# Sixty-four-row products for scores and turned probabilities, and pooled keys without masks

## The chip, the cores and the metric

The kernel runs on one core of one Trainium2 chip. The time is the device time of one launch in microseconds (us), a median over runs. Engines are named as the profile names them: PE is the matrix engine (a matmul is a weight load, on row PEld, and a stream of columns, on row PE), DVE the vector engine, ACT the scalar engine, POOL the general-purpose engine, SP the engine that issues most transfers.

## The reference

Three stages follow each other: attention over pooled keys and values, a weighted sum of four expert networks, and a gated network. Only the first is touched by the change.

```python
def _attn_ref(q, k, v):                      # (4, 8, 576, 64) each
    B, H, S, D = q.shape
    pool = 8
    Sp = S // pool                           # 72
    scale = 1.0 / np.sqrt(D)
    k_p = k.reshape(B, H, Sp, pool, D).mean(axis=3)
    v_p = v.reshape(B, H, Sp, pool, D).mean(axis=3)
    scores = scale * np.matmul(q, k_p.transpose(0, 1, 3, 2))
    scores = scores - np.max(scores, axis=-1, keepdims=True)
    attn = np.exp(scores)
    attn = attn / (np.sum(attn, axis=-1, keepdims=True) + 1e-09)
    return np.matmul(attn, v_p).astype(np.float32)

x = attn_out.transpose(0, 2, 1, 3).reshape(2304, 512)
x = _moe_ref(x, ...)                         # 4 experts, 512 -> 1024 -> 512
return _moe2_ref(x, ...)                     # two gates, a product, two more matmuls
```

## The kernel before

The 2304 tokens are worked on as 18 tiles of 128 (`t`), three tiles to a block of 384 (`i`, six blocks). A batch has 576 tokens, so tiles 4 and 13 hold the end of one batch and the beginning of the next; the helper `segments` cuts them in two halves of 64 tokens.

For a batch, `pool_k` sums eight rows of k for each of the 8 x 72 = 576 pooled rows, which lie in five chunks (`c`, four of 128 rows and one of 64), on DVE by one reduce or on POOL by three additions (the first four chunks of batch 1). The sum is then written twice side by side, once times a mask of even heads and once times a mask of odd heads (`mk`, made at the start); this is a product on POOL, or for three chunks of batch 1 a pair of scaled copies on ACT (`mask_k`). `make_kT` turns the chunks on PE, so that kT holds 128 rows: 64 rows of the even head above 64 rows of the odd head, with zeros where the head is not the column's. The last chunk of 64 rows is filled up with zeros to 128.

`scores(t)` (L530) then makes four products of 128 rows: the queries of a pair of heads are the weights (128 rows, 128 tokens) and 144 columns of kT stream through, 72 for each of the two heads. Heads 0 to 3 go into one PSUM bank and 4 to 7 into a second. The data are plain float32, and each product is two passes on PE (two weight loads and two streams): 8 passes for a whole tile, 16 for one that is cut in halves. `exps` takes the maximum of each bank on DVE and the exponential on ACT, `sums` and `normalise` follow, and `attn_T` (L575) turns the probabilities: eight transposes of 128 rows and 72 columns against the identity, one pass each, four into each of two banks, which ACT copies out (L578). `attend` (L587) multiplies with the pooled values: weights of 72 rows and 64 columns, two heads side by side in the two halves of the output's partitions. Its result is x, the input of the experts.

The order of the work is written out by hand. A list `lead` holds what runs before the first expert: pooling of batch 0, tiles 0 to 2 and their attend, the first weights. After that PE works on the experts' products (L174 to L176: three float32r passes of 384 or 512 columns), and `hooks` puts the rest of the attention between them: scores and exps of tile t at hook `at[t]`, its turn two hooks after the next tile's scores, attend of block i at the front of hook 10 i + 4, which is the hook of scores of tiles 7, 10, 13 and 16, so that these scores stand right behind an attend. The kT of batches 1, 2 and 3 stands at its own places. Everything of the attention is done by 180 us of the span; from there the experts go on, and then the gated network.

PSUM banks for the attention come from `bank`, a ring over eight banks that the experts' products use too.

Of the kernel before, what the change touches and what calls it, by code (L numbers as in the profile page):

```python
# [17 lines left out]
def fused_kernel(  # L18
# [16 lines left out]
    nc = tc.nc  # L35
# [295 lines left out]
    with tc.manual_schedule():  # L331
# [5 lines left out]
            ("at", (H // 2) * BLK * 4, 2), ("e", H * NK * 4, 3), ("kT", NCH * P * 4, 2), ("vp", H * D * 4, 2), ("qT", NP * P * 4, 1),  # L337
            ("kp", D * 4, 4), ("mx", H * 4, 2), ("sm", H * 4, 3), ("hm", NCH * H * 4, 1), ("mk", NCH * 2 * 4, 1),
# [14 lines left out]
        hm = ap.tile([P, NCH, H], F32, tag="hm", name="hm", bufs=1)  # L353
        nc.gpsimd.memset(hm, 1.0)
        nc.gpsimd.affine_select(out=hm, in_=hm, pattern=[[P, NCH], [-NK, H]], compare_op=ALU.is_ge,
                                fill=0.0, base=0, channel_multiplier=1)
        nc.gpsimd.affine_select(out=hm, in_=hm, pattern=[[-P, NCH], [NK, H]], compare_op=ALU.is_ge,
                                fill=0.0, base=NK - 1, channel_multiplier=-1)
        mk = ap.tile([P, NCH, 2], F32, tag="mk", name="mk", bufs=1)
        nc.vector.tensor_reduce(mk, hm.rearrange("p c (a b) -> p c b a", b=2), axis=AX.X, op=ALU.add)  # L360

# [49 lines left out]
        def pool_k(b, c, eng=nc.vector):  # L411
            if c == 0:
                kb_t[b] = ap.tile([P, NCH, 2, D], F32, tag="kb", name="kb", bufs=1)
            r, n = in_t.pop(("k", b, c))
            kp = ap.tile([P, D], F32, tag="kp", name="kp")
            if n < P and b == 0:
                nc.gpsimd.memset(kb_t[b][n:, c], 0.0)
# [18 lines left out]
        kp_t = {}  # L436

        def mask_k(c):
            for a in range(2):
                nc.scalar.activation(kb_t[1][:, c, a], kp_t[c], AF.Copy, scale=mk[:, c, a:a + 1])  # L440

        def make_kT(b, g0, g1):
# [8 lines left out]
            nc.scalar.activation(kT_t[b][:, g0 * P:g1 * P], pt[:, :(g1 - g0) * P], AF.Copy, scale=LOGIT)  # L451
# [71 lines left out]
        def scores(t):  # L523
            qT = qT_t.pop(t)
            sc_t[t] = []
# [136 lines left out]
        def weight(eng):  # L662
            return [(None, lambda: stream.split(eng))]
# [898 lines left out]
```

## Time and profile before

| what | value |
|---|---|
| median of 3 runs | 1148.17 us (1147.83 to 1148.45) |
| the profiled execution's own time | 1147.9 us |
| its span, first to last instruction | 1146.1 us |
| PE busy | 1139.6 us (99%) |
| DVE, POOL, ACT busy | 793.1, 416.8, 376.0 us |
| share of PE in the chain that ended last | 96% |
| granted TensorE clock in the 40 slices | full in all |

The profile gives the instructions of one execution. Starts of matmuls are recorded and their ends are modelled, so what a matmul costs in a row of them is read from the distance between starts. A row of the timeline gathers equal instructions that follow each other: with n of them, a duration d of the whole row and a duration s of one, the distance from start to start is (d - s) / (n - 1).

### The profile page before, as it was taken

Reading aid. Unit: us, or ns where it says so; the run is one execution under the profiler, and the core shown is the slowest. Engines: PE = TensorE matmul, PEld = TensorE weight load, DVE = VectorE, ACT = ScalarE, POOL = GpSimd, SP = SyncE. Lnnn points to the kernel's source line nnn. Section 1 sums busy time; section 2 is a strip of 40 time slices with the busy share of each in tenths; the row PEclk is TensorE's granted clock in tenths of the full one; section 3 lists DMA queues with packets and bytes.
Section 4 is the critical chain, followed back from the end, with each engine's and each line's share of the span. In section 5 each row is a group of like instructions: output and inputs, shape, how many; then the busy total and the mean of one; then the engine's idle time right before and its main releaser. Section 6 shows DMA issues by size and latency. Waiting matters only on the chain.

```text
span 1146.1 us, 17173 instructions
## 1 busy us (share of the span) xinstructions
PE 1139.6 (99%) x5985; PEld 1032.0 (90%) x5985; DVE 793.1 (69%) x1456; ACT 376.0 (33%) x672; POOL 416.8 (36%) x381
## 2 busy tenths in 40 slices
PE   8999999999999999999999999999999999999998
PEld 7898888999899898989898989989889999999997
DVE  7776544867768598658679578877786675774554
ACT  5643432345313053504134421314353313230110
POOL 6765213334525166524336642515001111331211
PEclk9999999999999999999999999999999999999999
DMA  9965515445966726495854578785476165947341
GB/s 229 229 148 123 186 62 197 166 152 183 322 220 196 235 80 181 142 316 167 263 152 123 182 237 192 238 208 146 145 195 230 43 261 209 333 152 288 112 166 56
DMA packets 211555, 213.85 MB, mean 187 GB/s; under 512 B 86596, under 2 KB 166796, under 8 KB 211468
## 3 DMA queue, kind: packets, MB, share of 16 engines
q1 hardware_dynamic: 211180, 212.23, 59.6%
q8 instruction: 47, 0.77, 0.3%
q10 hardware_dynamic: 288, 0.52, 0.1%
q14 instruction: 40, 0.33, 0.1%
HBM read 140.87 MB, written 71.83 MB: 186 GB/s over the span
## 4 chain that ended last, share of the span: by engine, by line
PE 96%; DVE 1%; POOL 1%; ACT 1%; DMA 0%; issue 0%; POOLq 0%
PE g L176 18%; PE g L174 18%; PE g L175 18%; PE s L174 13%; PE s L175 13%; PE s L176 13%; PE sc L530 1%; PE x_ps L587 1%; PE at_ps L575 1%; ACT ap L549 0%; DVE ap L419 0%; DMA stxh<-in_k_dram 0%; DVE ap L543 0%; POOL stxh L422 0%; POOL stxh L421 0%
## 5 line engine op out<-in xcount | busy, mean ns | idle before, releaser
L1014 DVE TENSOR_TENSOR plain<-s,plain 128x384 f32<-128x384 f32 x300 | 158.4, 554 | 83.5 <-PE s L176 35.4
L180 POOL TENSOR_TENSOR round<-x5l,round 128x768 fp32r<-128x768 f32 x60 | 112.2, 1870 | 271.5 <-ACT round L179 254.6
L176 PE MATMUL s<-xo,wl 128*128 128x384 f32 x624 | 208.6, 334 | 0.0
L174 PE MATMUL s<-xo,wh 128*128 128x384 f32 x624 | 208.6, 334 | 0.0
L175 PE MATMUL s<-xo,wh 128*128 128x384 f32 x624 | 208.5, 334 | 0.0
L174 PE MATMUL g<-w2l,round 128*128 128x512 f32 x522 | 204.8, 392 | 0.0
L176 PE MATMUL g<-w2h,round 128*128 128x512 f32 x522 | 203.8, 390 | 0.0
L175 PE MATMUL g<-w2h,round 128*128 128x512 f32 x522 | 203.5, 390 | 0.0
L174 PEld LDWEIGHTS s<-xo,wh 128*128 128x128 f32 x624 | 117.1, 188 | 0.5
L175 PEld LDWEIGHTS s<-xo,wh 128*128 128x128 f32 x624 | 117.1, 188 | 0.5
L176 PEld LDWEIGHTS s<-xo,wl 128*128 128x128 f32 x624 | 117.1, 188 | 0.0
L176 PEld LDWEIGHTS g<-w2h,round 128*128 128x128 f32 x522 | 97.9, 188 | 20.7
L174 PEld LDWEIGHTS g<-w2l,round 128*128 128x128 f32 x522 | 98.0, 188 | 20.0 <-issue 0.8
L175 PEld LDWEIGHTS g<-w2h,round 128*128 128x128 f32 x522 | 98.0, 188 | 19.4
L292 POOL TENSOR_TENSOR x5l<-x5l,x5h 128x256 uint32<-128x256 uint32 x80 | 60.6, 757 | 136.6 <-DVE x5h L291 128.3
L1018 ACT ACTIVATE plain<-s 128x384 f32<-128x384 f32 x60 | 29.2, 487 | 231.4 <-PE s L176 195.5
L179 ACT ACTIVATE round<-x5l 128x768 fp32r<-128x768 f32 x60 | 50.9, 848 | 147.7 <-DVE x5l L1422 146.6
L180 POOL TENSOR_TENSOR round<-plain,round 128x768 fp32r<-128x768 f32 (+1 forms) x29 | 52.5, 1812 | 117.7 <-ACT round L179 101.7
L286 DVE TENSOR_SCALAR x5l<-x5h 128x256 uint32<-128x256 uint32 x80 | 52.9, 662 | 50.3 <-DMA gate<-x5l 28.9
L1014 DVE TENSOR_TENSOR x5l<-s,plain 128x384 f32<-128x384 f32 x120 | 65.6, 556 | 24.8 <-PE s L176 18.3
L1260 ACT ACTIVATE plain<-plain 128x768 f32<-128x768 f32 x36 | 30.5, 848 | 111.3 <-DVE plain L1014 111.3
L174 PE MATMUL g<-xl,round 128*128 128x384 f32 x192 | 66.1, 344 | 0.0
(257 smaller groups left out, 2211.8 us busy)
## 6 DMA issues: line engine op xcount, KB each, us to landing
xo<-keptx SPq DMA_DIRECT2D x42, 768.0 KB
raw<-in_moe_w_dram SPq DMA_DIRECT2D x54, 256.0 KB
keptx<-xo SPq DMA_DIRECT2D x12, 768.0 KB
x5h<-in_moe_w_dram SPq DMA_DIRECT2D x128, 64.0 KB
x5h<-in_moe_w_dram SPq DMA_DIRECT2D x32, 256.0 KB
ob<-acc SPq DMA_DIRECT2D x24, 256.0 KB
kept<-xo SPq DMA_DIRECT2D x8, 768.0 KB
xo<-kept SPq DMA_DIRECT2D x8, 768.0 KB
```

What stands on the lines that cost most here:

```text
L174: nc.tensor.matmul(ps, lh, rl, start=first, stop=False)
L175: nc.tensor.matmul(ps, lh, rh, start=False, stop=False)
L176: nc.tensor.matmul(ps, ll, rh, start=False, stop=last)
L179: nc.scalar.activation(hi, src, AF.Copy)
L180: (lo_eng or nc.vector).tensor_tensor(lo, src, hi.bitcast(F32), op=ALU.subtract)
L286: nc.vector.tensor_scalar(au, h, 0x7FFFFFFF, None, op0=ALU.bitwise_and)
L292: nc.gpsimd.tensor_tensor(au, au, l, op=ALU.add)
L530: nc.tensor.matmul(sc[off:off + n, (hp % 2) * W:(hp % 2 + 1) * W], qT[:, hp, off:off + n], kT_t[b][:, hp * W:(hp + 1) * W], start=True, st ...
L575: nc.tensor.transpose(pt[:NK, g * P:(g + 1) * P], e[:, half * G + g, :], ident)
L1014: nc.vector.tensor_tensor(to, one, two, op=ALU.add)
L1018: nc.scalar.activation(x, product(j, A11, B11), AF.Copy)
L1260: nc.scalar.activation(r, r, AF.Relu)
```

## The change

The masks go. `pool_k` adds in three steps on either engine (256, 128 and twice 64 columns), and the last step writes the sum twice side by side, unmasked. `mask_k` and its copies on ACT go, and the products with the mask. kT therefore holds the same 64 rows twice, and the last chunk is turned with its 64 rows alone (64 rows of weights, 64 columns of identity).

`scores(t)` makes eight products of 64 rows: even heads from partitions 0 to 63 into one bank, odd heads from partitions 64 to 127 into the other, 72 columns each, in turn. `attn_T(t)` makes sixteen transposes of 64 rows: the first 64 tokens of a head into one bank, the last 64 into the other, in turn, 64 columns of identity each. Both banks of a tile are therefore filled together. The order of heads in the probabilities becomes even heads, then odd heads, and `attend` reads it so. The turn of a tile is now one piece; the line that put half of tile 4's turn one hook later goes.

```diff
-            ("at", (H // 2) * BLK * 4, 2), ("e", H * NK * 4, 3), ...
-            ("kp", D * 4, 4), ("mx", H * 4, 2), ("sm", H * 4, 3), ("hm", NCH * H * 4, 1), ("mk", NCH * 2 * 4, 1),
+            ("at", H * BLK * 4, 1), ("e", H * NK * 4, 3), ...
+            ("mx", H * 4, 2), ("sm", H * 4, 3),
...
         def pool_k(b, c, eng=nc.vector):
...
-            if eng is nc.vector:
-                eng.tensor_reduce(kp[:n], r[:n, :].rearrange("p (r d) -> p d r", d=D), axis=AX.X, op=ALU.add)
-            else:
-                eng.tensor_tensor(r[:n, :256], r[:n, :256], r[:n, 256:], op=ALU.add)
-                eng.tensor_tensor(r[:n, :128], r[:n, :128], r[:n, 128:256], op=ALU.add)
-                eng.tensor_tensor(kp[:n], r[:n, :64], r[:n, 64:128], op=ALU.add)
-            if b == 1 and c < NCH - 2:
-                kp_t[c] = kp
-                return
-            (eng if b == 1 else nc.gpsimd).tensor_tensor(kb_t[b][:n, c], kp[:n].unsqueeze(1).broadcast_to([n, 2, D]),
-                                    mk[:n, c].unsqueeze(2).broadcast_to([n, 2, D]), op=ALU.mult)
+            kb = kb_t[b][:n, c]
+            for m in (256, 128):
+                eng.tensor_tensor(r[:n, :m], r[:n, :m], r[:n, m:2 * m], op=ALU.add)
+            one, two = (r[:n, m:m + D].unsqueeze(1).broadcast_to([n, 2, D]) for m in (0, D))
+            eng.tensor_tensor(kb, one, two, op=ALU.add)
...
-        def mask_k(c):
-            for a in range(2):
-                nc.scalar.activation(kb_t[1][:, c, a], kp_t[c], AF.Copy, scale=mk[:, c, a:a + 1])
...
             for c in range(g0, g1):
-                nc.tensor.transpose(pt[:, (c - g0) * P:(c - g0 + 1) * P],
-                                    kb_t[b][:, c].rearrange("p a d -> p (a d)"), ident)
+                n = min(P, NROW - c * P)
+                nc.tensor.transpose(pt[:, (c - g0) * P:(c - g0) * P + n],
+                                    kb_t[b][:n, c].rearrange("p a d -> p (a d)"), ident[:n, :n])
...
         def scores(t):
-            for half in range(2):
-                sc = bank("sc")
-                for hp in range(2 * half, 2 * half + 2):
-                    for off, n, b, s in segments(t * P, P):
-                        nc.tensor.matmul(sc[off:off + n, (hp % 2) * W:(hp % 2 + 1) * W],
-                                         qT[:, hp, off:off + n], kT_t[b][:, hp * W:(hp + 1) * W],
+            sc_t[t] = [bank("sc") for _ in range(2)]
+            for hp in range(NP):
+                for off, n, b, s in segments(t * P, P):
+                    for a, sc in enumerate(sc_t[t]):
+                        nc.tensor.matmul(sc[off:off + n, hp * NK:(hp + 1) * NK], qT[a * D:(a + 1) * D, hp, off:off + n],
+                                         kT_t[b][a * D:(a + 1) * D, (2 * hp + a) * NK:(2 * hp + a + 1) * NK],
                                          start=True, stop=True)
...
-        def attn_T(t, half):
+        def attn_T(t):
...
-            pt = bank("at_ps")
-            for g in range(G):
-                nc.tensor.transpose(pt[:NK, g * P:(g + 1) * P], e[:, half * G + g, :], ident)
...
+            pts = [bank("at_ps") for _ in range(2)]
+            R = P // 2
+            for g in range(H):
+                for n, pt in enumerate(pts):
+                    rows = slice(n * R, (n + 1) * R)
+                    nc.tensor.transpose(pt[:NK, g * R:(g + 1) * R], e[rows, g, :], ident[rows, rows])
...
-        hooks[at[TPB + 2] + 3][:0] = [hooks[at[TPB + 2] + 2].pop()]
```

In the lead, PE's rows from the first scores to the attend of block 0 (sc are the banks of scores, at_ps those of the turned probabilities, vp_ps sums of values, x_ps the attend), before:

```order
L530 MATMUL sc<-ap_72,plain 128x144 x4
L509 MATMUL qT_ps<-ident,stxh 128x128 x4
L530 MATMUL sc<-ap_72,plain 128x144 x8
L469 MATMUL vp_ps<-stxl,ident 72x192 x8
L575 MATMUL at_ps<-ident,ap_72 72x128 x8
L469 MATMUL vp_ps<-stxl,ident 72x64 x8
L575 MATMUL at_ps<-ident,ap_72 72x128 x16
L587 MATMUL x_ps<-ap_72 64x384 x8
```

And after:

```order
L505 MATMUL sc<-ap_72,plain 128x72 x8
L485 MATMUL qT_ps<-ident,stxh 128x128 x4
L505 MATMUL sc<-ap_72,plain 128x72 x16
L445 MATMUL vp_ps<-stxl,ident 72x192 x8
L552 MATMUL at_ps<-ident,ap_72 72x64 x16
L445 MATMUL vp_ps<-stxl,ident 72x64 x8
L552 MATMUL at_ps<-ident,ap_72 72x64 x32
L564 MATMUL x_ps<-ap_72 64x384 x8
```

No group has moved; scores and turns have twice the products, each with half the columns.

Among the experts, PE's rows around the kT of batch 1 (kT_ps; the g are the experts' banks), before:

```order
L174 MATMUL g_491<-xl,round 128x384
L175 MATMUL g_491<-xh,round 128x384
L176 MATMUL g_491<-xh,round 128x384
L447 MATMUL kT_ps<-ident,plain 128x128 x5
L174 MATMUL g_524<-w2l,round 128x512
```

And after:

```order
L174 MATMUL g_525<-xl,round 128x384
L175 MATMUL g_525<-xh,round 128x384
L176 MATMUL g_525<-xh,round 128x384
L422 MATMUL kT_ps<-ident,plain 128x128 x4
L422 MATMUL kT_ps<-ident,plain 128x64
L174 MATMUL g_558<-w2l,round 128x512
```

The last of the five transposes has become one of 64 rows, in the same place.

On ACT, between the attend of block 0 (xh) and the exponentials of tile 3, before (L440 is `mask_k`):

```order
L179 ACTIVATE xh<-x_ps 128x384 x4
L179 ACTIVATE round<-raw 128x512
L440 ACTIVATE plain<-ap_72 128x64 x2
L745 ACTIVATE round<-g_408 128x384
L179 ACTIVATE round<-raw 128x512
L179 ACTIVATE w2h<-raw 128x512
L440 ACTIVATE plain<-ap_72 128x64 x4
L549 ACTIVATE ap_72<-sc,ap_72 128x72 x8
```

And after:

```order
L179 ACTIVATE xh<-x_ps 128x384 x4
L179 ACTIVATE round<-raw 128x512
L720 ACTIVATE round<-g_441 128x384
L179 ACTIVATE round<-raw 128x512
L179 ACTIVATE w2h<-raw 128x512
L523 ACTIVATE ap_72<-sc,ap_72 128x72 x8
```

The six masked copies are gone from in front of the exponentials, and with them ACT's wait for the pooling on POOL.

## Rows read from the trace of the kernel before

**Rows 1.** From the page: span, PE's busy time, the chain that ended last.
```profile
span 1146.1 us, 17173 instructions
...
PE 1139.6 (99%) x5985; PEld 1032.0 (90%) x5985; DVE 793.1 (69%) x1456; ACT 376.0 (33%) x672; POOL 416.8 (36%) x381
...
PE 96%; DVE 1%; POOL 1%; ACT 1%; DMA 0%; issue 0%; POOLq 0%
```

**Rows 2.** Groups by line and shape, PE: count, busy us, mean ns of one.
```profile
L575 PE MATMUL at_ps<-ident,ap 128*72 128x128 f32 x144 | 18.8, 272 | 0.2 <-ACT ap L549 0.2
L530 PE MATMUL sc<-ap 128*128 128x144 f32 x104 | 15.5, 291 | 0.2 <-ACT ap L578 0.2
...
L469 PE MATMUL vp_ps<-stxl,ident 72*72 72x64 f32 x16 | 1.2, 227 | 0.0
```

**Rows 3.** Timeline of PE: scores at 111 us, turn at 116 us (start, length).
```profile
111.00 0.39 PE L176 MATMUL g<-w2h,round 128*128 128x512 f32 x1
111.23 1.14 PE L530 MATMUL sc<-ap 128*128 128x144 f32 x8
...
116.41 1.03 PE L575 MATMUL at_ps<-ident,ap 128*72 128x128 f32 x8
...
117.51 0.40 PE L175 MATMUL g<-w2h,round 128*128 128x512 f32 x1
```

**Rows 4.** Timeline of PE: an attend, then scores of the cut tile 13.
```profile
119.11 0.39 PE L176 MATMUL g<-w2h,round 128*128 128x512 f32 x1
119.43 2.80 PE L587 MATMUL x_ps<-ap 72*64 72x384 f32 x16
122.06 1.15 PE L530 MATMUL sc<-ap 128*64 128x144 f32 x16
...
123.47 0.39 PE L175 MATMUL g<-w2h,round 128*128 128x512 f32 x1
```

**Rows 5.** Timeline of PEld, the weight loads, in the same stretch.
```profile
119.42 0.20 PEld L587 LDWEIGHTS x_ps<-ap 72*64 72x64 f32 x4 [0.35 <-issue]
119.80 0.14 PEld L587 LDWEIGHTS x_ps<-ap 72*64 72x64 f32 x2 [0.18 <-issue]
120.12 0.14 PEld L587 LDWEIGHTS x_ps<-ap 72*64 72x64 f32 x2 [0.18 <-issue]
...
123.14 0.19 PEld L174 LDWEIGHTS g<-w2l,round 128*128 128x128 f32 x1 [0.20 <-issue]
123.25 0.19 PEld L175 LDWEIGHTS g<-w2h,round 128*128 128x128 f32 x1
```

**Rows 6.** Timeline of PE: sums of values in the lead, weights of 72 columns.
```profile
17.44 1.20 PE L469 MATMUL vp_ps<-stxl,ident 72*72 72x64 f32 x16
```

**Rows 7.** Timeline of PE: the kT of batch 2.
```profile
78.75 0.71 PE L447 MATMUL kT_ps<-ident,plain 128*128 128x128 f32 x5
```

**Rows 8.** Timeline of the lead and after: pooling of k, first scores, what POOL waits for.
```profile
4.41 2.92 DVE L419 TENSOR_REDUCE ap<-stxh 128x64 f32<-128x512 f32 x3 [2.10 <-DMA stxh<-in_k_dram]
...
9.27 0.39 POOL L427 TENSOR_TENSOR plain<-ap 64x128 f32<-64x128 f32 x1 [0.27 <-DVE ap L419]
...
10.44 1.22 PE L530 MATMUL sc<-ap,plain 128*128 128x144 f32 x8
...
11.21 0.95 DVE L543 TENSOR_REDUCE ap<-sc 128x4 f32<-128x288 f32 x2 [0.91 <-PE sc L530]
...
13.62 0.72 POOL L461 TENSOR_TENSOR stxl<-stxl 72x256 f32<-72x256 f32 x1 [0.88 <-DMA stxl<-in_v_dram]
...
16.86 1.15 POOL L566 TENSOR_TENSOR ap<-ap 128x576 f32<-128x576 f32 x1 [0.48 <-DVE ap L561]
...
26.89 0.69 DVE L180 TENSOR_TENSOR round<-raw,round 128x512 fp32r<-128x512 f32 x1
...
28.67 0.59 ACT L440 ACTIVATE plain<-ap 128x64 f32<-128x64 f32 x2 [0.82 <-POOL ap L423]
...
30.20 0.28 DVE L427 TENSOR_TENSOR plain<-ap 64x128 f32<-64x128 f32 x1
```

More of the change, by code (lines that the diff above doesn't have):

```diff
@@ L350, in bank @@
             return spare[(turn[0] - 1) % len(spare)](name)
[L353 to L360, printed above, removed]
         staging = [home.tile([P, 3, 512], F32, tag=f"x{i}{t}", name="stx" + t) for i in (NB - 1, NB - 2, NB - 3) for t in "hl"]
@@ L412, in pool_k @@
             if c == 0:
-                kb_t[b] = ap.tile([P, NCH, 2, D], F32, tag="kb", name="kb", bufs=1)
+                kb_t[b] = ap.tile([P, NCH, 2, D], F32, tag="kb", name="kb")
             r, n = in_t.pop(("k", b, c))
-            kp = ap.tile([P, D], F32, tag="kp", name="kp")
-            if n < P and b == 0:
-                nc.gpsimd.memset(kb_t[b][n:, c], 0.0)
-            if eng is nc.vector:
-                eng.tensor_reduce(kp[:n], r[:n, :].rearrange("p (r d) -> p d r", d=D), axis=AX.X, op=ALU.add)
-            else:
-                eng.tensor_tensor(r[:n, :256], r[:n, :256], r[:n, 256:], op=ALU.add)
-                eng.tensor_tensor(r[:n, :128], r[:n, :128], r[:n, 128:256], op=ALU.add)
-                eng.tensor_tensor(kp[:n], r[:n, :64], r[:n, 64:128], op=ALU.add)
-            if b == 1 and c < NCH - 2:
-                kp_t[c] = kp
-                return
-            (eng if b == 1 else nc.gpsimd).tensor_tensor(kb_t[b][:n, c], kp[:n].unsqueeze(1).broadcast_to([n, 2, D]),
-                                    mk[:n, c].unsqueeze(2).broadcast_to([n, 2, D]), op=ALU.mult)
+            kb = kb_t[b][:n, c]
[3 more added lines that the diff above has]
+            eng.tensor_tensor(kb, one, two, op=ALU.add)
         warm_ps = []
@@ L566, in normalise @@
                 eng.tensor_tensor(e_t[t][:, some], e_t[t][:, some], sm_t[t][:, some].unsqueeze(2).broadcast_to([P, h[1] - h[0], NK]), op=ALU.mult)
-        def attn_T(t, half):
+        def attn_T(t):
             i, o = divmod(t, TPB)
             if o == 0:
-                at_t[i, half] = ap.tile([P, G, BLK], F32, tag="at", name="at")
+                at_t[i] = ap.tile([P, H, BLK], F32, tag="at", name="at")
             e = e_t[t]
-            pt = bank("at_ps")
-            for g in range(G):
-                nc.tensor.transpose(pt[:NK, g * P:(g + 1) * P], e[:, half * G + g, :], ident)
-            src = pt[:NK].rearrange("p (g s) -> p g s", s=P)
-            dst = at_t[i, half][:NK, :, o * P:(o + 1) * P]
-            nc.scalar.activation(dst, src, AF.Copy)
+            pts = [bank("at_ps") for _ in range(2)]
[4 more added lines that the diff above has]
+                    nc.tensor.transpose(pt[:NK, g * R:(g + 1) * R], e[rows, g, :], ident[rows, rows])
+            for n, pt in enumerate(pts):
+                at = o * P + n * R
+                nc.scalar.activation(at_t[i][:NK, :, at:at + R], pt[:NK].rearrange("p (g s) -> p g s", s=R), AF.Copy)
         def attend(i, hp):
@@ L587, in attend @@
                     nc.tensor.matmul(px[a * D:(a + 1) * D, off:off + n], vp_t[b][:NK, 2 * hp + a],
-                                     at_t[i, hp // 2][:NK, 2 * (hp % 2) + a, off:off + n], start=True, stop=True)
+                                     at_t[i][:NK, a * G + hp, off:off + n], start=True, stop=True)
             hi_lo(xh[:, hp, :], xl[:, hp, :], px[:, :BLK])
@@ L638, in do_turn @@
         def do_turn(t):
-            return [(None, lambda half=half: attn_T(t, half)) for half in range(2)]
+            return [(None, lambda: attn_T(t))]
         def do_attend(i):
@@ L694, in fused_kernel @@
                 + do_turn(1) + do_turn(2)
-                + do_qT(3) + k1[:4] + do_attend(0) + [(None, lambda: rest_of_q.pop(0)())] + weight(VE) + [(None, lambda: mask_k(0)), (None, lambda: rest_of_q.pop(0)())])
+                + do_qT(3) + k1[:4] + do_attend(0) + [(None, lambda: rest_of_q.pop(0)())] + weight(VE) + [(None, lambda: rest_of_q.pop(0)())])
         V1 = 5
@@ L699, in fused_kernel @@
         hooks[1] = k1[4:] + do_qT(TPB + 1)
-        hooks[0] = [(None, lambda c=c: mask_k(c)) for c in range(1, NCH - 2)]
         at = {TPB: 0, TPB + 1: 5, TPB + 2: 8}
```

8 lines of the change are left out of this document (3 added, 5 removed).

## Prediction

> **What bounds the kernel now.** I read the page first: PE is busy 1139.6 of 1146.1 us, and 96% of the chain that ended last is PE [rows 1]. A busy PE need not be a fast one, so I then looked at starts. In the stretch where the attention lies between the experts' products the matmuls follow each other at the distance of their columns: a 512-column pass every 0.23 us, the scores without a gap behind it [rows 3]. PE's waits for the attention's banks are 0.2 us in each group [rows 2]. So from about 25 us on, each us that the change adds to or takes from PE is a us of the kernel. Before that, in the lead, DVE, POOL and transfers set the pace [rows 8].
>
> What the steps cost on PE, read from starts: the 8 passes of scores take (1.14 - 0.29) / 7 = 0.122 us each, 0.98 in all; the 8 transposes (1.03 - 0.27) / 7 = 0.108 each, 0.87 in all [rows 2, 3]. Both are 0.84 ns for a column. After the transposes PE goes on at once: 116.41 + 0.87 + 0.23 = 117.51, where the second expert pass stands [rows 3].
>
> **What shows how narrow products behave.** The trace has no product of 64 rows. It has products of 64 weight columns, which fill half of the array: the attend and the scores of the cut tile. There two things are seen.
>
> First, neighbours in different halves run together: 16 passes of 384 columns take 2.80 us, where 16 x 384 x 0.84 ns would be 5.2, and 16 passes of the cut tile take what 8 of a whole tile take [rows 3, 4].
>
> Second, going over to them and back costs. After the 512-column pass at 119.11 the next should start at 119.34. The first narrow load starts at 119.42, and pairs stand 0.32 apart from 119.80 on, so the first pair began in effect at 119.48: 0.08 to 0.09 us in which PE empties, and 0.06 for a load that nothing covers [rows 4, 5]. On the way back the last pair of scores starts at 122.06 + 7 x 0.122 = 122.92 and is streamed at 123.04; the load comes at 123.14, a second one 0.11 later, and the pass at 123.47 puts the first at 123.24 [rows 4, 5]. That is 0.10 for emptying and 0.10 for the load. Between full shapes neither is seen.
>
> The Trainium skill (TensorEngine Tiling (Array Packing), Key Properties) says that a change of the tiling mode drains the engine, and lists tiles of 64 rows as such a mode. The trace bears that out for half columns, 0.09 us; for half rows no row here shows it. By that rule the sum below holds; without a drain it is that of the second rival.
>
> **Loads.** With half the columns to stream, the load may be what is left. The sums of values stream 64 columns (0.054 us at 0.84 ns) behind loads of 72 columns, and their starts are (1.20 - 0.23) / 15 = 0.065 apart [rows 2, 6]: there the load sets the pace. Two loads of 128 columns stand 0.11 apart [rows 5]. A load's time goes by its columns, and the change halves rows of weights: the scores still load 128 tokens, the turns 72 keys. So I take 0.11 us for a pair of new score passes (stream 0.06) and 0.065 for a pair of new transposes (stream 0.054). From below, if loads did not bind, the streams; from above, if the two halves did not run together, twice these.
>
> **The change, part by part, on PE.** Tiles 3 to 17 lie in the stretch that PE bounds.
>
> Scores of a whole tile alone (tiles 3, 5, 6, 8, 9, 11, 12, 14, 15, 17): in 0.09 + 0.11, eight pairs 7 x 0.11 + 0.06 = 0.83, out 0.20: 1.23 against 0.98 to 0.99. +0.24 x 10 = +2.4.
>
> Scores right behind an attend (7, 10, 16): the attend's way out, 0.20, is paid now as well, so 1.19 becomes 0.10 + 0.11 + 0.83 + 0.20 = 1.24. +0.05 x 3 = +0.15.
>
> Cut tiles (4, 13): quarter products, 32 passes. Four at a time: 8 x 0.062 = 0.50 against 0.98; two at a time: 1.0. Tile 13 shares its mode with the attend now and then no longer does, +0.15. I take the middle: -0.3.
>
> Turns (15 tiles): in 0.09 + 0.06, eight pairs 7 x 0.065 + 0.055 = 0.51, out 0.20: 0.86 against 0.87. Nothing.
>
> kT of batches 1 to 3: the last transpose, 0.11 now ((0.71 - 0.29) / 4 [rows 7]), becomes one of 64 rows: 0.09 + 0.11 + 0.055 + 0.20 = 0.455. +0.345 x 3 = +1.0.
>
> Sum +3.25. Most of it is the way in and out: 28 trips of some 0.35 to 0.40, more than 10 us, against 7 us that half-height products save. The unknown is therefore the trip; if it cost seven tenths of what it costs for half columns, the sum would be nil.
>
> **The lead.** A reduce of k takes 2.92 / 3 = 0.97 us on DVE. The three additions: 512 columns take 0.69 and 128 take 0.28, so 256 take 0.42, and 0.42 + 0.28 + 0.28 = 0.98, each needing the one before [rows 8]. Nothing over five chunks; bounds -0.9 (starts overlapping by 0.06 each) and +0.5. The product with the mask on POOL, 0.39 with its hand-over 0.45, goes [rows 8]. Against that the 64-row kT and its way out, and the way into the scores, add some 0.4, and the first maximum, which now starts when one bank is done (11.21 for scores from 10.44), waits for both, +0.4. So it comes 0.35 later, bounds -0.6 and +0.9. It reaches the experts only in part: POOL pools a v that lands at 13.62 whatever k does, then normalises tile 0; tile 1 waits 0.48 for DVE at 16.86 and would wait 0.35 more [rows 8].
>
> Behind the lead ACT is relieved: six masked copies, of which the last pair waits 0.82 for POOL and ends at 29.26, stand before the exponentials of tile 3 [rows 8]. Without them these start up to 0.5 earlier, and what PE waits for behind them shrinks by some 0.3. POOL's last addition grows from 64 to 128 columns, off PE's path as long as the kT of batch 1 is not late; its product with the mask goes there too. Pooling of batches 2 and 3, on DVE and POOL, is hidden under PE and counts nothing; if that cover went it would be ten times 0.01 on DVE. The turn of tile 4 in one piece, and banks that must both be free at once, put back a few tenths of waiting. Lead and waits together: 0, bounds -1 and +1.5.
>
> **Sum.** 1146.1 + 3.25 in the span, 1.8 around it as now, and 0.27 by which the median of the runs stands above the profiled 1147.9: 1151.4. With trips from 0.30 to 0.45 and the bounds above, this case reaches from 1149 to 1155.
>
> **Rivals.**
> *The load hides in the drain.* The next weights come in while PE empties, and a trip costs two drains, 0.19. For it: between full shapes a load comes early, the one at 123.25 well before its pass at 123.47 [rows 4, 5]. Against it: in both trips of rows 4 and 5 the load stands behind the drain. 28 trips save 0.16 to 0.22 each, 5.3 us: 1146.1.
> *No drain for half rows* (the other side). Rows of the array are cut, not its outputs, and PE runs on as between full shapes. For it: weights of 72 rows cost no trip [rows 6]. Against it: those fill more than half, and half columns do drain. Then scores save 8 x 0.01 x 13 = 1.0 to 1.3, cut tiles 0.5, turns 8 x 0.043 x 15 = 5.2, kT nothing: -7.0, 1141.2. This wins wherever a trip is under 0.1.
> *Twice as fast.* Neither loads nor drains bind, and scores and turns halve: (0.49 + 0.43) x 15 = 13.8 less, 1134.4. The 0.065 of rows 6 speaks against it. The Trainium skill (TensorEngine Tiling (Array Packing), Theoretical Speedup) gives up to this factor for a small dimension of 64; no run here shows it for half rows.
> *Halves do not run together.* Two row halves write to the same partitions of two banks, which half columns do not. Then 16 passes of 0.11 for scores, 16 of 0.065 for turns: +1.1 x 13 + 1.1 x 2 + 0.52 x 15 + 1.0 = 25, 1173.
> The change does what it says: the new order has the pairs next to each other.
>
> **How the numbers follow.** The forecast 0.50; load hidden 0.17; no drain 0.22; twice 0.03; not together 0.05; the rest, a lead that loses more, 0.03. About 0.2%, 2.3 us, is what can be told from no change. Of the forecast's chance 0.33 lies above 1150.5, 0.16 within, 0.01 below; of the load's 0.10 below and 0.07 within; the next two are faster, the last two slower. Faster 0.36, same 0.23, slower 0.41. The range from 1140.5 to 1155 holds nearly all of the forecast and the load's case and most of no drain, 0.84; both signs are in it, and the forecast's own range is 1149 to 1155.
>
> **What would show it.** In the profile after: sixteen score passes in pairs a few ns apart, pairs 0.11 apart (0.06 if loads don't bind); transposes in pairs 0.065 apart; the load of the first expert pass behind them about 0.10 after the last stream, as at 123.14 now; the 64-row kT standing 0.35 us longer. If the load behind a turn starts before its stream ends, the drain is refuted and the time is near 1141. If pairs don't exist, it is near 1173. If the first expert pass comes later than now by more than half a us, the lead was mis-sized.

## The result, and the profile after

The changed kernel takes 1155.27 us (median of 4 runs, 1154.33 to 1156.77), the kernel before beside it 1148.04 us: a ratio of 1.0064, 95% interval 1.0046 to 1.0081. It is 7.2 us slower. The sign is the forecast's; the time is 3.9 us above it and 0.27 us above the end of its range.

The page of the kernel after, from a profiled execution of 1155.39 us, has the span, PE's busy time and the chain that ended last, as [rows 1] for the kernel before:

```profile
span 1153.6 us, 17782 instructions
...
PE 1144.3 (99%) x6289; PEld 1026.0 (89%) x6289; DVE 798.4 (69%) x1486; ACT 374.9 (32%) x666; POOL 410.4 (36%) x361
...
PE 95%; DVE 3%; DMA 1%; SPq 1%; ACT 0%; issue 0%; DVEq 0%
```

The span has grown by 7.5 us, PE's busy time by 4.7, and DVE has 3% of the chain where it had 1%. So PE did more, but there are also new stretches in which it waits. The new lines are L505 for scores (before L530), L552 for turns (L575), L555 for ACT's copy behind a turn (L578), L564 for the attend (L587), L422 for kT (L447), L406 and L408 for the pooling of k (L419, L427), L517 and L525 for the maximum and the subtraction on DVE (L543, L551).

**Shapes.** Timeline of PE in the kernel after (start, length of the row): scores of a tile, a kT, a turn, each with the expert pass behind it, and the load of that pass.

```profile
73.73 1.11 PE L505 MATMUL sc<-ap 64*128 64x72 f32 x16
74.78 0.50 PE L174 MATMUL g<-w2l,round 128*128 128x512 f32 x1
...
82.35 0.80 PE L422 MATMUL kT_ps<-ident,plain 128*128 128x128 f32 x5
83.08 0.44 PE L174 MATMUL g<-xl,round 128*128 128x384 f32 x1
...
122.87 0.49 PEld L552 LDWEIGHTS at_ps<-ident,ap 64*72 64x72 f32 x16 [0.25 <-POOL ap L439]
122.87 0.64 PE L552 MATMUL at_ps<-ident,ap 64*72 64x64 f32 x16
123.44 0.19 PEld L174 LDWEIGHTS g<-w2l,round 128*128 128x128 f32 x1
```

The two of a pair start 7 ns apart in the scores and 4 to 5 ns apart in the turns, so the row halves run together. Pairs of scores stand 0.112 apart, pairs of transposes 0.056. A turn without waits takes from 122.87 to the load at 123.44, 0.57. The row of kT has grown by 0.09 in itself ([rows 7] has 0.71) and by more behind it. In the cut tiles the quarter products run four at a time. This is tile 4 of the kernel after:

```profile
38.25 0.73 PE L505 MATMUL sc<-ap 64*64 64x72 f32 x32
```

Its passes start in fours, 7 ns apart within a four and 0.062 from one four to the next.

What a group costs PE between two expert passes (from where the one before ends, its start plus 0.173 or 0.227, to where the one behind begins in effect), worked out from the starts; medians of groups without a wait (tile 4 waits in the kernel before, so its price there is that of `turns_only`, which has the same products in that place; the forecast for a cut tile is the middle between four and two at a time):

| group | before | after | difference | forecast | count |
|---|---|---|---|---|---|
| scores alone | 0.98 | 1.254 | +0.27 | +0.24 | 10 |
| scores behind an attend, with it | 3.93 | 4.00 | +0.07 | +0.05 | 3 |
| turn | 0.88 | 0.78 | -0.10 | 0 | 15 |
| kT | 0.555 | 0.84 | +0.285 | +0.345 | 3 |
| attend and cut tile 13 | 3.91 | 3.59 | -0.32 | -0.08 | 1 |
| cut tile 4 alone | 1.34 | 0.87 | -0.47 | -0.23 | 1 |

**The lead and the clock.** The attend of block 0, which ends the lead, in the kernel before and, with expert passes behind it, in the kernel after; a bracket holds the wait and what ended it:

```profile
20.72 2.80 PE L587 MATMUL x_ps<-ap 72*64 72x384 f32 x16 [0.33 <-ACT ap L578]
```

```profile
21.76 4.02 PE L564 MATMUL x_ps<-ap 72*64 72x384 f32 x16 [1.17 <-ACT ap L555]
25.71 0.69 PE L174 MATMUL g<-xl,round 128*128 128x384 f32 x1
26.19 0.53 PE L175 MATMUL g<-xh,round 128*128 128x384 f32 x1
...
29.39 0.53 PE L176 MATMUL g<-xh,round 128*128 128x384 f32 x1
```

Before, the attend started at 20.72 after a wait of 0.33, took 2.80, and the twelfth expert pass, the last ahead of the scores of tile 3, started at 25.47. Now PE waits 1.17 for ACT, starts 1.04 later, and the attend takes 4.02. The expert passes of 384 columns stand (29.39 - 26.19) / 10 = 0.32 apart, where they stand 0.173 apart elsewhere. The windows say why (us, busy time of PE, PEld, DVE, ACT and POOL with the instructions, granted clock, DMA share, GB/s). Before:

```profile
20.00:25.00 5.00, 4.67 (x29) 2.74 (x28) 3.71 (x6) 4.03 (x10) 4.68 (x8) 1.00 0.96 312
25.00:30.00 5.00, 5.00 (x33) 5.00 (x32) 4.17 (x7) 3.42 (x14) 4.54 (x8) 1.00 1.11 212
```

After:

```profile
20.00:25.00 5.00, 3.71 (x27) 1.53 (x24) 2.25 (x4) 2.95 (x6) 4.69 (x9) 0.82 0.93 313
25.00:30.00 5.00, 5.00 (x18) 3.86 (x14) 2.07 (x3) 1.09 (x4) 4.55 (x8) 0.50 0.61 136
```

From 20 to 25 PE was busy 3.71 us, before 4.67; most of the difference is the wait of 1.17. In that stretch the granted clock fell from 2.4 to 1.2 GHz. At 0.82 in one window and 0.50 in the next, it was low for (1 - 0.82) x 5 / 0.5 = 1.8 and 5 us, 6.8 in all. It rose again while PE was busy without a gap. In the 40 slices of the page every slice still reads 9, which stands for 90% or more: a slice is 29 us long.

**New waits.** PE's waits in the attention of the kernel after (what waits for what; us in total, times, longest), where the kernel before had 0.2 or 0.3 once for each:

```profile
PE at_ps L552 <- DVE ap L525: 1.6, 3, 0.7
PE x_ps L564 <- ACT ap L555: 1.2, 1, 1.2
```

The first row is two turns, near 79 and near 111 us. The timeline of the second, DVE, POOL and PE in one:

```profile
102.89 1.55 DVE L406 TENSOR_TENSOR stxh<-stxh 128x256 f32<-128x256 f32 x2
103.14 1.15 POOL L540 TENSOR_TENSOR ap<-ap 128x576 f32<-128x576 f32 x1 [11.20 <-ACT ap L555]
...
104.47 0.70 DVE L408 TENSOR_TENSOR plain<-stxh 128x128 f32<-128x128 f32 x1
...
106.30 1.42 DVE L406 TENSOR_TENSOR stxl<-stxl 128x256 f32<-128x256 f32 x2
...
110.26 0.46 DVE L525 TENSOR_TENSOR ap<-sc,ap 128x288 f32<-128x288 f32 x1
...
110.86 0.22 PE L552 MATMUL at_ps<-ident,ap 64*72 64x64 f32 x1 [0.71 <-DVE ap L525]
```

The scores were there at 105.8, but DVE came to their maximum at 109.78, behind four chunks of k. The first transpose starts 0.14 after the first bank of scores has been read (110.26 + 0.46), the others 0.14 after the second. By the program this is because the turn gets the banks of the scores: behind the lead the kernel cuts the list of banks to two (`spare[:] = spare[:2]`, in both kernels). The sentence ahead of the prediction that speaks of a ring over eight banks holds for the lead alone.

And the first two additions of a chunk, and the third, which in the lead take this,

```profile
5.66 0.74 DVE L406 TENSOR_TENSOR stxh<-stxh 128x256 f32<-128x256 f32 x2
...
6.43 0.29 DVE L408 TENSOR_TENSOR plain<-stxh 128x128 f32<-128x128 f32 x1
```

take 1.55, 0.88, 1.42 and 1.42 in the four chunks, and the third addition up to 0.70, while POOL works beside them. Before, three reduces of k ran beside POOL as well, in the same place:

```profile
99.68 3.03 DVE L419 TENSOR_REDUCE ap<-stxl 128x64 f32<-128x512 f32 x3
...
101.25 1.15 POOL L566 TENSOR_TENSOR ap<-ap 128x576 f32<-128x576 f32 x1
```

They took 3.03, in the lead 2.92 [rows 8]. It is the operation with two inputs that POOL slows.

### The profile page after: what moved, and what is told of

The parts are those of the page before. It is cut to its first block, busy times and chain, and to the rows that moved or that the text cites. A ratio compares the mean times of both kernels' runs of the same rounds, so it can differ in the third digit from the quotient of the medians.

```text
span 1153.6 us, 17782 instructions
## 1 busy us (share of the span) xinstructions
PE 1144.3 (99%) x6289; PEld 1026.0 (89%) x6289; DVE 798.4 (69%) x1486; ACT 374.9 (32%) x666; POOL 410.4 (36%) x361
## 4 chain that ended last, share of the span: by engine, by line
PE 95%; DVE 3%; DMA 1%; SPq 1%; ACT 0%; issue 0%; DVEq 0%
PE g L174 18%; PE g L176 18%; PE g L175 18%; PE s L174 13%; PE s L176 13%; PE s L175 13%; PE x_ps L564 2%; PE sc L505 1%; PE at_ps L552 1%; DMA raw<-in_moe_w_dram 1%; DVE stxl L406 0%; DVE stxh L406 0%; SPq L454 0%; DMA stxl<-in_v_dram 0%; DVE ap L525 0%
## 5 line engine op out<-in xcount | busy, mean ns | idle before, releaser
L286 DVE TENSOR_SCALAR x5l<-x5h 128x256 uint32<-128x256 uint32 x80 | 49.6, 620 | 48.7 <-DMA gate<-x5l 26.6
```

The costliest lines, as they stand in the source:

```text
L286: nc.vector.tensor_scalar(au, h, 0x7FFFFFFF, None, op0=ALU.bitwise_and)
```

## The experiments

The theory is a sum: the shapes as in the table, a lead about 1 us longer, some 3 us of low clock that follow from it, and 2.0 us of waits behind DVE's additions. Its rivals give one of these another cause or another size; each expectation names its own.

A table of delays serves for all. The experts' products are the same 5460 passes in every kernel, so the start of the n-th pass minus its start in the kernel before tells where time was lost (us, profiled execution of each):

| pass (its start before) | after | warm | reduce | base | base_fullkT | scores_only | turns_only | turns_late |
|---|---|---|---|---|---|---|---|---|
| 1 (23.45) | 2.25 | 1.02 | 2.81 | 1.01 | 0.56 | 0.53 | 1.97 | 0.53 |
| 12 (25.47) | 3.92 | 1.02 | 4.27 | 1.00 | 0.55 | 0.53 | 3.64 | 0.54 |
| 101 (48.70) | 3.77 | 0.84 | 3.87 | 1.55 | 0.97 | -0.11 | 3.51 | 1.08 |
| 201 (78.05) | 3.60 | 0.65 | 3.25 | 0.94 | 0.35 | 0.81 | 2.28 | -0.16 |
| 301 (106.45) | 5.81 | 2.82 | 3.86 | 1.55 | 0.66 | 3.02 | 1.96 | -0.47 |
| 601 (187.56) | 6.26 | 3.29 | 4.36 | 2.04 | 0.87 | 4.15 | 1.30 | -1.13 |

### The clock: warm

The kernel after, with ten transposes of the identity into the attend's bank while PE waits for ACT. They add nothing to the result.

```diff
+            if i == 0 and hp == 0:
+                turn_ident(px, 10)
```

> The changed kernel with ten extra transposes of the identity on PE in front of the attend of block 0 (their result is overwritten), where PE stood idle for 1.3 us at 20.4 to 21.8 us. Theory A: that idle time is what lets the granted clock fall to half from 23.1 to 29.9 us in the profile after, and the low clock costs 3 us of the 7.2: then the clock stays full and the time is 1152 to 1153. Theory B: the low clock lies under the waits of the lead and costs nothing, PE would wait for the first experts anyway: then 1155 whatever the clock does.

It took 1152.5 us (1151.31 to 1153.43), ratio 1.0031 [1.002, 1.0043], against 1.0064 without them. Timeline of PE of this kernel, and its windows:

```profile
20.50 1.31 PE L414 MATMUL x_ps<-ident 128*128 128x128 f32 x10
21.74 2.80 PE L566 MATMUL x_ps<-ap 72*64 72x384 f32 x16
...
26.49 0.34 PE L176 MATMUL g<-xh,round 128*128 128x384 f32 x1
```

```profile
20.00:25.00 5.00, 4.88 (x39) 2.92 (x38) 2.81 (x5) 3.34 (x7) 4.69 (x9) 1.00 0.99 303
25.00:30.00 5.00, 5.00 (x40) 4.68 (x38) 3.85 (x8) 2.22 (x6) 4.69 (x7) 1.00 0.95 176
```

The attend starts at the same time, 21.74, but takes 2.80 again, and the clock stays at 2.4 GHz. The twelfth pass starts at 26.49 where it was 29.39: the low clock cost 2.9 us up to there, and 0.25 more in the scores of tile 3 behind it (1.50 for 1.25). 1.0 us of the lead remains.

### The waits on DVE: reduce, base

The kernel after, with k of batches 2 and 3 pooled by one reduce as before and copied twice by POOL; the three additions stay for batches 0 and 1.

```diff
+            if b >= 2:
+                kp = ap.tile([P, D], F32, tag="kp", name="kp")
+                eng.tensor_reduce(kp[:n], r[:n, :].rearrange("p (r d) -> p d r", d=D), axis=AX.X, op=ALU.add)
+                nc.gpsimd.tensor_copy(kb, kp[:n].unsqueeze(1).broadcast_to([n, 2, D]))
+                return
```

> The changed kernel with the pooling of k for batches 2 and 3 as before on DVE (one reduce) and a copy on POOL that writes the sum twice, without a mask. Theory A: the three additions on DVE take up to twice as long while POOL works (1.42 us for the first two against 0.74 alone), hold up the exponentials behind them, and PE waits 0.44 us at the turn near 79 us and 1.6 us near 110 us for that: then these waits go and the time is 1153.2, 2 us below the change. Theory B: the waits come from both banks being taken at once by scores and turns: then they stay, and so does the time, 1155.

The two turns took 0.771 and 0.780 where they had taken 1.218 and 2.378, 2.0 us less, and in PE's waits the row on DVE L525 is gone; the 1.2 of the attend is there still.

The whole moved less: 1154.82 us, ratio 1.0054 [1.0041, 1.0066], 0.8 less than after when each stands against the kernel before beside it. The low clock was there still. The attend starts at 21.76 as in the kernel after, but the clock fell 0.6 earlier (granted 0.76 and 0.55 in the two windows), and the twelfth pass came 4.27 late where it came 3.92 late in the kernel after. How long the clock is low differs between executions: its mean over an execution is 0.995 to 0.999 in the four of the kernel after and 0.995 to 0.997 in the five of `reduce`. At 0.997 the kernel after took 1155.39 and 1155.15, `reduce` 1153.90 and 1154.76; the median execution of `reduce` stands at 0.995. So a part of the gain is hidden by the clock. Whether that is all of it was not settled by this kernel; where the clock doesn't interfere, the gain shows better. `base` is the kernel after with both edits, warm's and reduce's:

> The changed kernel with the ten extra transposes in the lead and with the pooling of batches 2 and 3 by one reduce, both as in the runs before: what is left should be the products' shapes and the later lead alone. If the two causes add up, 2.0 below the run with the extra transposes: 1150.5. If they are one cause seen twice (the waits near 79 and 110 us only move), 1152.5.

1150.97 us (1149.82 to 1152.2), ratio 1.0025 [1.0016, 1.0033]; that is 1.3 us less than warm, when each stands against the kernel before beside it. The two edits together take away 4.4 of the 7.2 us.

### The parts alone: scores_only, turns_late, turns_only

`scores_only` is the kernel after with the old turns of 128 rows. `turns_late` is the kernel before with the new turns from tile 3 on, `turns_only` with the new turns from tile 0 on; they have the old scores and the old pooling. The edits exchange `attn_T` whole, as in the diff of the change, so only the line that tells the last two apart is given:

```diff
+            if t < 3:
+                return [(None, lambda half=half: attn_T_full(t, half)) for half in range(2)]
             return [(None, lambda: attn_T(t))]
```

> The changed kernel with the turns as before: eight transposes of 128 rows, four into each bank, ACT copying the first bank while the second is filled. Theory A (PE's shapes): a lone group of turns takes 0.78 us of PE in the change and 0.88 before, so 15 turns cost 1.5 more and late waits stay; in the lead the turn of tile 2 is done earlier by 0.5 us and the idle time in front of the first attend shrinks, so the low clock may not come: 1153 with the clock full, 1156.5 if it falls as now. Theory B (the new turns are the loss, by their way in and out): 1150.

> The kernel before with the new turns of 64 rows alone, from tile 3 on; tiles 0 to 2, scores, pooling and masks as before. Theory A (PE's shapes): each of the 15 turns takes 0.10 us less of PE, nothing else changes: 1146.5, 1.5 us below before. Theory B (by the prediction's sum, a pair of transposes 0.065 us apart and a way in and out of 0.35): no change, 1148.

> The kernel before with the new turns alone, in all tiles, those of the lead too; scores, pooling and masks as before. Theory A: in the lead both banks of tile 2's turn are done together, ACT's copies and the first attend come 0.5 us later, and PE stands idle longer in front of it, so that the granted clock may fall as in the change: 1149.8 if it does, 1147.3 if not, against 1146.9 with the new turns from tile 3 on. Theory B: the lead is late because of the scores and the pooling of k, the turns have no part in it: 1146.9.

`scores_only`: 1153.91 us, ratio 1.0044 [1.0032, 1.0057], nearer to the 1153 of its theory A than to the 1150 of B. The clock stays high, turns are back at 0.88, and the wait behind DVE is there (a turn of 2.08 near 108 us).

`turns_late`: 1147.02 us (1145.84 to 1147.93), ratio 0.9985 [0.9976, 0.9994]. It is the one kernel of this study whose interval lies below 1. Fifteen turns at 0.10 less are 1.5 us, and the table has 0.53 + 1.13 = 1.7 between the first and the 601st pass. The new turns are a gain, if a small one, in the stretch that PE bounds.

`turns_only`: 1149.16 us, ratio 1.0009 [1.0000, 1.0018]. Only the three turns of the lead are added, and it loses 2.4 us, when each stands against the kernel before beside it. Its attend and its windows:

```profile
21.77 3.72 PE L590 MATMUL x_ps<-ap 72*64 72x384 f32 x16 [1.16 <-ACT ap L581]
```

```profile
20.00:25.00 5.00, 3.71 (x27) 1.44 (x24) 2.57 (x5) 3.10 (x7) 4.69 (x9) 0.85 0.95 309
25.00:30.00 5.00, 5.00 (x17) 4.58 (x16) 1.87 (x3) 1.81 (x5) 4.49 (x9) 0.50 0.85 190
```

These are the late attend and the low clock of the kernel after, without its scores and its pooling. So the turn in the lead brings them. Before, four transposes fill the first bank, and ACT copies it while PE fills the second; the attend's first products need the first copy alone. Now both banks are filled by the last transposes, ACT's two copies (0.54 each) come one after the other behind them, and the attend waits for both. ACT's copies in the kernel before and after, of which the last two are those of tile 2:

```profile
19.61 1.55 ACT L578 ACTIVATE ap<-at_ps 72x512 f32<-72x512 f32 x3
```

```profile
20.63 1.08 ACT L555 ACTIVATE ap<-at_ps 72x512 f32<-72x512 f32 x2 [0.20 <-PE at_ps L552]
```

Before, the attend starts at 20.72, while the last copy is still at work; now it starts at 21.76, behind the end of both at 21.71. In the middle of the kernel an attend comes long after its turn, and nothing waits.

The executions of `turns_only` also show what the clock is worth. At a mean granted clock of 0.999 one of the eleven took 1147.28 us, close to `turns_late`; nine at 0.996 or 0.997 took 1148.68 to 1149.92, and one at 0.995 took 1150.26.

The pass table also warns. `turns_late` has the lead of the kernel before, and still reached its first pass 0.53 later; three kernels further down with that same lead, `turns_mid`, `turns_pair` and `turns_front`, reached it 0.04, 0.54 and 0.90 later. So the 1.0 us by which the lead of the kernel after is longer can't be told from the scatter between executions by the pass alone. What can be told is the wait ahead of the attend: 0.30 to 0.33 in these four and in the kernel before, 1.16 or 1.17 in after, reduce and turns_only, some 0.85 more.

### The trip itself: turns_mid, turns_front, base_fullkT

The prediction's main term is the way from passes of 128 rows to passes of 64 and back. `turns_mid` is `turns_late` with one more pass of 128 rows in the middle of each of the 15 turns, into columns that are written again later; `turns_front` has the same pass ahead of the turn (`g == 0` in place of `g == G`).

```diff
+                if g == G:
+                    nc.tensor.transpose(pts[0][:, 3 * P:], ident, ident)
```

> The kernel before with the new turns from tile 3 on (turns_late), and one more pass of all 128 rows (an identity transpose into columns that the last two pairs write again) in the middle of each of the 15 turns. Theory A (each way from passes of all rows to passes of 64 rows and back costs a fixed trip): a turn of 0.78 us has 8 pairs of 0.056, 0.45, so 0.32 is the trip; the pass adds itself, 0.11, and a second trip of 0.32: turns of 1.21 us, 15 x 0.43 = +6.4 on turns_late's 1147.0, about 1153.4. Theory B (the 0.32 is the fill and the end of any group between expert passes, whatever its rows): the pass adds 0.11 alone, turns of 0.89, +1.6, about 1148.6.

> The same pass of all 128 rows, but as the first instruction of each of the 15 turns, where PE comes from passes of all rows anyway. Both theories: turns of 0.78 + 0.11 = 0.89 us, 15 x 0.11 = +1.6, about 1148.6. If theory A holds, turns_mid stands 4.8 us above this kernel; under B the two are alike.

`turns_mid` took 1151.86 us, ratio 1.0032 [1.002, 1.0043]; `turns_front` 1147.85 us, ratio 0.9995 [0.9986, 1.0004]. They do the same work and differ by 4.0 us, 0.27 for a turn. That refutes theory B; theory A, with a trip of 0.32, had asked for 1153.4 and 4.8 us. Timeline of PE, `turns_mid` and then `turns_front`:

```profile
76.64 0.42 PE L580 MATMUL at_ps<-ident,ap 64*72 64x64 f32 x8
76.99 0.33 PE L577 MATMUL at_ps<-ident 128*128 128x128 f32 x1
77.25 0.42 PE L580 MATMUL at_ps<-ident,ap 64*72 64x64 f32 x8
77.59 0.44 PE L174 MATMUL g<-xl,round 128*128 128x384 f32 x1
```

```profile
106.17 0.27 PE L577 MATMUL at_ps<-ident 128*128 128x128 f32 x1
106.37 0.64 PE L580 MATMUL at_ps<-ident,ap 64*72 64x64 f32 x16
106.94 0.50 PE L174 MATMUL g<-w2l,round 128*128 128x512 f32 x1
```

From the first transpose to the expert pass it is 0.95 against 0.57. The medians of all turns are 1.161, 0.885 and, without the pass, 0.779: ahead of the turn the pass costs 0.106, its 128 columns; in its middle 0.276 more. That is the trip, there and back, and it exists for halves of the rows. Why it is 0.05 less than the 0.33 that the turns alone give below is open. The tiling rule of the Trainium skill (TensorEngine Tiling (Array Packing), Key Properties), that a change of mode drains the engine, agrees with these 0.276 us; what a drain costs the page doesn't say.

`base_fullkT` is base with the last transpose of each kT of 128 rows again, its spare rows set to zero once.

```diff
-                n = min(P, NROW - c * P)
-                nc.tensor.transpose(pt[:, (c - g0) * P:(c - g0) * P + n],
-                                    kb_t[b][:n, c].rearrange("p a d -> p (a d)"), ident[:n, :n])
+                nc.tensor.transpose(pt[:, (c - g0) * P:(c - g0 + 1) * P],
+                                    kb_t[b][:, c].rearrange("p a d -> p (a d)"), ident)
```

> base (the changed kernel with ten idle transposes ahead of the first attend and the one-input pooling of batches 2 and 3) with the last transpose of each kT of all 128 rows again (batch 0's 64 spare rows are set to zero once). Theory A (the 64-row transpose at the end of kT costs a trip): three kT groups of 0.84 us go back to 0.55, 3 x 0.285 = -0.86 from base's 1151.0, about 1150.1; groups of the first 200 us unchanged but for kT. Theory B (kT's groups grew for another cause, such as the copies behind them): no change in the groups and 1151.0.

The kT groups went from 0.84 back to 0.553; the row of one reads as in [rows 7]:

```profile
79.10 0.71 PE L428 MATMUL kT_ps<-ident,plain 128*128 128x128 f32 x5
```

Three times 0.289 is 0.87. The median, 1150.56 us, ratio 1.0019 [1.001, 1.0028], is 0.6 below base when each stands against the kernel before beside it; the interval doesn't tell that from 0.87, the groups do.

### Two attempts to share a trip: base_together, turns_pair

If a trip costs 0.28, groups of 64 rows should stand together. `base_together` puts nine of base's turns directly in front of the scores of two tiles further on; `turns_pair` puts the first two turns of each block of `turns_late` one behind the other. The first two lines of the diff are those of `base_together`, the last that of `turns_pair`.

```diff
+            if t % TPB != TPB - 1 and t + 2 < NTILE:
+                hooks[at[t + 2]][:0] = do_turn(t)
...
+            hooks[at[t + 2 if t % TPB == 0 else t + 1] + 2] += do_turn(t)
```

> The same kernel with the turn of nine tiles put directly in front of the scores two tiles on, so that PE goes over to half rows and back once for both. Theory A (the trip is the price of half rows): each of the nine saves one way out, 0.20, and one way in, 0.10 to 0.20, together 2.7 to 3.6: 1147.3, slightly below the kernel before. Theory B (the time lies in the narrow passes, not in the trip): no change, 1150.5.

> The kernel before with the new turns from tile 3 on, and with the first two turns of each block of three made one behind the other at the place of the second: five trips less. Theory A (the trip costs 0.115 in and 0.20 out): 1.6 below the same kernel with single turns, 1145.3. Theory B (the trip is hidden or the four copies on ACT come too late for what follows): 1146.9 or above.

Neither saved anything. That ACT's copies could come too late was theory B of `turns_pair`; `base_together` had no such theory. `base_together` took 1164.2 us, ratio 1.0149 [1.0129, 1.0168], `turns_pair` 1155.26 us, ratio 1.0061 [1.0048, 1.0074]. One row of PE's waits in `base_together`, the first such place and a window of it (columns as above), and one row of the waits in `turns_pair`:

```profile
PE sc L510 <- ACT ap L560: 7.2, 9, 1.6
```

```profile
44.44 1.86 PE L510 MATMUL sc<-ap 64*128 64x72 f32 x16 [1.58 <-ACT ap L560]
```

```profile
45.00:50.00 5.00, 5.00 (x25) 4.17 (x26) 2.76 (x6) 2.53 (x16) 4.69 (x8) 0.66 0.97 207
```

```profile
PE at_ps L578 <- ACT ap L581: 5.2, 9, 1.6
```

With two banks for the attention the second group needs the banks that the first has just filled, and PE stands still until ACT has copied them. Waits of 0.7 to 1.6 us stand against a saving of 0.28: in `base_together` turn and scores together take 3.04 to 3.10 in the later places and 4.47 in the first, where apart they take 0.78 and 1.25. Behind the first such wait the granted clock was low for some 3.4 us (0.66 in the window). The row of scores took 1.86 there and 1.59 in the next place, where the clock was high, with a second, shorter wait inside the row; without waits it takes 1.11. A part of the 1164.2 is the clock: the four executions took 1161.84 to 1167.76, the two slower ones at a mean granted clock of 0.996 and 0.993, the others at 0.998 and 0.999. So these two kernels tell nothing of trips; they tell that the distance between groups is what pays for having two banks.

## Why the prediction was right and wrong, step by step

**Right: the half rows run together, and going over to them costs a trip.** The mechanism of the forecast stood; the rivals without a drain, twice as fast and not together are refuted by the 7 ns within pairs, by scores that cost more than before and by `turns_mid`. That the load hides in the drain is refuted too: the first load behind the turn of 122.87 comes at 123.44, 0.09 behind the stream of its last pair, which starts at 123.30 and lasts 0.054. By the working of the sum (a group less its seven distances between pairs and its last stream) a trip is 1.254 - 0.78 - 0.06 = 0.41 in the scores, 0.33 in the turns and 0.289 + 0.109 - 0.054 = 0.34 in kT, where the sum had 0.40, 0.35 and 0.40; `turns_mid` puts that of the turns at 0.28.

**Right: scores, kT.** +2.7 for +2.4, +0.2 for +0.15, +0.86 for +1.0.

**Mis-sized: the turns, -1.5 where the sum had 0.** The step that failed is "0.065 for a pair of new transposes", taken from the sums of values [rows 6]. The pairs stand 0.056 apart, the time of their 64 columns: 7 x 0.009 = 0.06 of the 0.08 between 0.86 and 0.78, and the trip gives the rest. The loads of the two lines in the kernel before (count, busy us, mean ns of one) could have hinted at it:

```profile
L575 PEld LDWEIGHTS at_ps<-ident,ap 128*72 128x72 f32 x144 | 15.7, 115 | 2.4 <-ACT ap L549 0.4
L469 PEld LDWEIGHTS vp_ps<-stxl,ident 72*72 72x72 f32 x32 | 3.4, 144 | 0.3
```

With the same 72 columns the transposes' loads take 115 ns and those of the sums 144. I took the price from the sums because their stream had 64 columns, and the load's row of the line itself was not read.

**Mis-sized: the cut tiles, -0.8 where the sum had -0.3.** "I take the middle" was the step. By the prediction's own working four at a time gives -0.48 for tile 4 and -0.33 for tile 13, and four at a time is what came: -0.47 and -0.32.

**Mis-sized: waits near tiles 3 to 6.** I put the wait that PE is spared at 0.3. The group of the scores of tile 4 took 1.73 in the kernel before, where it is 1.34 without a wait (`turns_only`). The timeline of the kernel before has this row,

```profile
33.50 1.61 PE L530 MATMUL sc<-ap 128*64 128x144 f32 x16
```

where the same sixteen products take 1.15 in tile 13 [rows 4]. With what PE waited in the turn of tile 3 (1.26 for 0.88), in the scores of tile 5 (1.23 for 0.98) and in half a turn and the scores of tile 6 behind it (1.88 for 1.42) it is 1.5 us. Much of that was probably gone after because PE was late anyway: in base, which reaches these tiles earlier, the turn of tile 3 takes 1.59, 0.8 of it a wait. No run tests this alone.

**Wrong: "the lead and waits together: 0, bounds -1 and +1.5".** I followed k through the lead, chunk by chunk, and that was right to a few tenths: the first maximum comes at 11.65 where it came at 11.21, 0.44 later for my 0.35. What I did not follow is the end of the lead: turn 2, ACT's copies, attend. The end of the lead moved by up to 1.04, and the clock made 3.9 of it. That PE, at 2.4 GHz in every slice, could lose its clock there was in no rival. My condition, that a first expert pass more than half a us late means a mis-sized lead, was met; the price behind it was three times the delay. Together the term came to about +4.6: lead 1.0, clock 3.1, new waits 2.0, waits spared -1.5.

**Wrong: "pooling of batches 2 and 3 ... is hidden under PE ... if that cover went it would be ten times 0.01 on DVE".** The cost was 2.0 us. I compared 0.98 of additions with 0.97 of reduce, both by rows of DVE alone, and did not ask what POOL does beside them, nor what stands behind them in DVE's queue: the maximum of scores that hold the banks of the next turn. The trace of before had the price. DVE's subtraction of two inputs takes 0.69 at 26.89 [rows 8], where POOL's next addition starts behind it; at 33.53, with POOL at work since 33.17, the same form takes this:

```profile
33.53 1.47 DVE L180 TENSOR_TENSOR round<-raw,round 128x512 fp32r<-128x512 f32 x1
```

The Trainium skill (SBUF — State Buffer, SBUF: two separate sides) says that a DVE operation with two SBUF inputs and a POOL operation that reads SBUF exclude each other: the one that starts first keeps the other out for its whole instruction. The rows here agree: the second addition of the chunk at 102.89 starts at 103.29, while POOL is busy until 104.29, and ends at 104.44, 0.15 behind it. In the two later chunks the same addition ends 0.15 behind POOL again, at 107.72 for 107.57 and at 109.46 for 109.31.

**The account.** From the table of delays, at the 601st pass: 3.92 until the twelfth pass (1.0 lead, 2.9 clock), 0.25 of low clock in the scores of tile 3, shapes +2.7 + 0.2 + 0.86 - 1.5 - 0.8 = +1.5, new waits +2.0, waits spared -1.5; 6.2 against 6.26 measured. The profiled execution lost another 1.2 far behind the attention, about 0.75 of it near 969 us, where PE waits for a chain over ACT and DVE. `reduce` shows this loss too and base doesn't; why the chain came late is open, and so is about 1 us of the 7.2. With clock and DVE's waits taken out, base is at 1150.97, close to the forecast of 1151.4. That is partly luck: turns and cut tiles gave 2.0 more, and the lead took up to 1.0 more, than the sum said.

## What to carry to other kernels

Before an operation is exchanged for another "of the same length", look at what runs beside it on DVE or POOL, and at who waits behind it in the queue. Where a step fills two buffers in turn in place of one after the other, nobody can begin on the first early: at the seam where the consumer stands right behind, this cost 0.85 us of waiting and, through the clock, some 3 more, while in the middle of the kernel the same edit gained 1.5. Narrow products next to wide ones pay a trip (here 0.28 to 0.41 us), so count groups, not products, and check that there are buffers enough before putting groups together.

## What the runs showed of the chip beyond this

Ten transposes that compute nothing made the kernel 3.1 us faster, each measured against the kernel before beside it: they stand in a wait of 1.17 us, and without them the granted clock fell to 1.2 GHz for 6.8 us, from 23.2 on. `turns_only` and `reduce` have the wait and lost their clock as well, in each of their executions; warm and base, where the transposes fill it, and `turns_late`, which waits 0.3 there, kept theirs in all.

POOL is slowed by DVE as DVE is by POOL. In the kernel before POOL's addition of 128 columns takes 0.46 at 29.41 and 0.87 at 27.03, where DVE's subtraction of 26.89 to 27.58 stands ahead of it:

```profile
27.03 0.87 POOL L422 TENSOR_TENSOR stxh<-stxh 128x128 f32<-128x128 f32 x1
...
29.41 0.46 POOL L422 TENSOR_TENSOR stxl<-stxl 128x128 f32<-128x128 f32 x1
```

Why a load of 72 columns takes 115 ns in one line and 144 in another was not tried.
